# Output product by Strassen's seven quarter products in place of eight, on even and odd tokens, from column 512 on; x in a ring of block tiles

## The chip, the cores and the metric

One core of a Trainium2 chip. Its engines run side by side and meet through semaphores: TensorE (PE, with its weight loads PEld), VectorE (DVE), ScalarE (ACT), GpSimd (POOL) and SyncE (SP), which issues most transfers. The metric is the device time of one execution, in microseconds (us). Times given are medians of several runs.

## The reference

q, k and v are (8 batches, 8 heads, 576 positions, 64). A retention layer without a softmax gives x, 4608 tokens by 512, and a gated feed-forward layer gives the output, 4608 by 512 in float32:

```python
scores = scale * np.matmul(q, k.transpose(0, 1, 3, 2))
gamma = 1.0 - 2.0 ** (-5.0 - np.arange(H, dtype=np.float32))
Dmat = np.where(rel >= 0, gamma[:, None, None] ** rel[None, :, :], 0.0)   # rel = i - j
ret = scores * Dmat[None, :, :, :]
x = np.matmul(ret, v).transpose(0, 2, 1, 3).reshape(B * S, H * D)
gate = 1.0 / (1.0 + np.exp(-(x @ w_gate)))      # w_gate, w_val: 512 by 1536
val = x @ w_val
out = (gate * val) @ w_out                       # w_out: 1536 by 512
```

## The kernel before, in words

Matmuls take bf16 operands and add up in f32 in PSUM. x is held transposed, features on partitions and tokens along columns (`xT`). The kernel puts the tokens in an order of its own: a step of attention makes 128 columns of `xT`, and `rows` maps columns back to rows of the output.

The order of the work is written out by hand, and each engine's queue runs in that order. Columns 0 to 511 are made first, together with the loading and casting of the weights. From column 512 on a loop runs over `BLOCKS`: one of 256 columns, called block 512 after its first column, two of 384 (768 and 1152), and six of 512 (1536 to 4096). A block has two phases:

- *The hidden phase* (`h_units`). For each of 12 chunks of 128 hidden units, matmuls with `w_gate` and `w_val` (L734, four each) fill PSUM, ScalarE takes the sigmoid `g` (L748 in block 512, L758 after it), and VectorE multiplies to `gv` (L750, L762), which is bf16. The tiles come from `ffn_psum`, a ring of three banks: a chunk can start when the engine that reads the bank's old contents is done. In block 512 a chunk fills one bank, later it fills two.
- *The output phase* (`op_units`). For each 128 tokens, 12 matmuls of 512 columns with `wo_sb` (L801) add up in one bank; ScalarE copies it to `ob` (L777), and SP stores it later (L772). The last tile of the kernel is split in three parts (L791 to L796).

Between these units stands the attention of later columns. Up to block 1152 mostly single steps (`next_slot`) stand in the hidden phases; from there on double steps (`next_two`) stand in the output phases, at a fixed number of units from their start. A step has matmuls for its scores and state products (L519, L527) and for the values of an earlier step (L545, L561); VectorE masks the scores (L534), adds the states (L646, L642, L648) and, for single steps, adds one half of x (L633); ScalarE casts states (L495) and evacuates x (L603, L619). `glance` (L589) is a copy of one column, which makes TensorE's last value matmuls wait until VectorE has come to it. `pending` holds what is to follow a step, one entry per unit. In early block 512 a transpose on TensorE (L480) with copies on ScalarE and VectorE (L482) also stands; a copy of two small states (`sf`, L677) belongs to the fourth step.

q, k and v of later steps are loaded by SP in `ld_pool`, a ring of 18 buffers, and cast by GpSimd (L291, L296) at least three steps ahead of their use; most are then transposed by a transfer.

Of the kernel before, what the change touches and what calls it, by code (L numbers as in the profile page):

```python
# [9 lines left out]
FP32 = mybir.dt.float32  # L10
BF16 = mybir.dt.bfloat16
# [5 lines left out]
def kernel(  # L17
# [35 lines left out]
    att_pool = ctx.enter_context(tc.tile_pool(name="att", bufs=3))  # L53
    nat_pool = ctx.enter_context(tc.tile_pool(name="nat", bufs=5))
    consts = ctx.enter_context(tc.tile_pool(name="consts", bufs=1))

# [4 lines left out]
    st_psum = ctx.enter_context(tc.tile_pool(name="st_psum", bufs=1, space=PS))  # L61
    ffn_psum = ctx.enter_context(tc.tile_pool(name="ffn_psum", bufs=3, space=PS))

# [194 lines left out]

    xT = consts.tile([P, M, NT], BF16)


    natural = {}
# [171 lines left out]
    def third_out(apart):  # L434

        ps = pair_ps[5][0][0]
        share = nat_pool.tile([P, 2, P], FP32, tag="apart", name="apart", bufs=1)
        nc.vector.tensor_copy(out=share, in_=apart)
        nc.vector.tensor_tensor(out=xT[:, 0:2, 5 * P:6 * P], in0=ps[:, 0:2], in1=share, op=ALU.add)
        nc.scalar.copy(out=xT[:, 2:4, 5 * P:6 * P], in_=ps[:, 2:4])  # L440

# [23 lines left out]
    def pair_out(A, a, *engs):  # L465
        t0 = (2 * A + a) * P
        k = M // len(engs)
        for i, eng in enumerate(engs):
            ps, at_m, _ = pair_ps[2 * A + a][i * k]
            eng(out=xT[:, i * k:(i + 1) * k, t0:t0 + P], in_=ps[:, at_m:at_m + k])  # L470

# [127 lines left out]
    def after_two(vals, news, i):  # L599

        if i < NJ:
            for s in vals:
                nc.scalar.copy(out=xT[:, :, cols_of(s, i)], in_=val_ps[s][i])  # L603
        for n, s in enumerate(news):
            b, c = STEPS[s]
            if c == LAST:
                continue
            if i == n:
                add_state(s, 0)
                add_state(s, 1)  # L610
            if i == n + 1:
                for j in range(NJ):
                    if (s, j) in totals:
                        keep_state((b, c, j), totals.pop((s, j)), on_act)

    def leave_own(s, j):

        own = slice(2 * j, 2 * j + 2)
        nc.scalar.copy(out=xT[:, own, cols_of(s, j)], in_=val_ps[s][j][:, own])  # L619

# [6 lines left out]
    def leave_other(s, j):  # L627

        other = slice(2 - 2 * j, 4 - 2 * j)
        if before(s, j) is None:  # L630
            nc.vector.tensor_copy(out=xT[:, other, cols_of(s, j)], in_=val_ps[s][j][:, other])
        else:
            nc.vector.tensor_tensor(out=xT[:, other, cols_of(s, j)], in0=val_ps[s][j][:, other], in1=shares.pop((s, j)),  # L633
                                    op=ALU.add)

# [83 lines left out]
    def h_units(gvs, fcs, t0, a, e, banks=None):  # L719
# [6 lines left out]
        for i0 in range(0, len(fcs), k):  # L726
# [5 lines left out]
            def mm(out, w_sb, fc):  # L732
                for kc in range(NKC):
                    nc.tensor.matmul(out, lhsT=w_sb[:, kc, fc * P:(fc + 1) * P],  # L734
                                     rhs=xT[:, kc, t0 + a:t0 + e],
                                     start=(kc == 0), stop=(kc == NKC - 1))
# [32 lines left out]
    def leave():  # L769
        r, ob = stores.pop(0)  # L770
        for p0, r0, w in rows(r, P):
            nc.sync.dma_start(out[r0:r0 + w, :], ob[p0:p0 + w])  # L772

    def store(opp, r0, eng=None):

        ob = osb_pool.tile([P, DM], FP32, tag="osb", name=f"ob_{r0}")
        (eng or on_act)(out=ob, in_=opp)  # L777
        stores.append((r0, ob))
        if len(stores) > KEEP:
            leave()  # L780

    def op_units(gvs, t0, n):
        for nb in range(n // P):
            r0 = t0 + nb * P
            if r0 == NT - P:

                for i, (c0, w, queue, eng) in enumerate(((0, 256, nc.sync, on_act), (256, 128, nc.sync, on_dve),
                                                         (384, 128, nc.scalar, on_act))):
                    opp = ffn_psum.tile([P, w], FP32, tag="ffn", name=f"op_{t0}_{nb}_{i}")
                    for fc in range(NFC):  # L790
                        nc.tensor.matmul(opp, lhsT=gvs[fc][:, nb * P:(nb + 1) * P], rhs=wo_sb[:, fc, c0:c0 + w],  # L791
                                         start=(fc == 0), stop=(fc == NFC - 1))
                    ob = osb_pool.tile([P, w], FP32, tag="osb", name=f"ob_{r0}_{i}")
                    eng(out=ob, in_=opp)
                    for p0, at_row, n_row in rows(r0, P):
                        queue.dma_start(out[at_row:at_row + n_row, c0:c0 + w], ob[p0:p0 + n_row])  # L796
                    yield 12 * w
                return
            opp = ffn_psum.tile([P, 512], FP32, tag="ffn", name=f"op_{t0}_{nb}")
            for fc in range(NFC):  # L800
                nc.tensor.matmul(opp, lhsT=gvs[fc][:, nb * P:(nb + 1) * P], rhs=wo_sb[:, fc, :],  # L801
                                 start=(fc == 0), stop=(fc == NFC - 1))
                if fc % 4 == 3 and fc < NFC - 1:
                    yield 4 * 512
            store(opp, t0 + nb * P)
            yield 4 * 512

    def ffn_units(t0, n):
        gvs = {}
        yield from h_units(gvs, range(NFC), t0, 0, n)  # L810
        yield from op_units(gvs, t0, n)

# [17 lines left out]
    def h_both(fcs):  # L830

        gs = {}
        for what in ("g", "v"):
            for fc in fcs:
                pool, tag = (qk_psum, "qk") if what == "g" else (ffn_psum, "ffn")
                ps = pool.tile([P, 512], FP32, tag=tag, name=f"h{what}_0_{fc}")
                for kc in range(NKC):
                    nc.tensor.matmul(ps, lhsT=(wg_sb if what == "g" else wv_sb)[:, kc, fc * P:(fc + 1) * P],  # L838
                                     rhs=xT[:, kc, 0:4 * P], start=(kc == 0), stop=(kc == NKC - 1))
                if what == "g":  # L840
# [63 lines left out]
    def h_half(what, fc, x, ps):  # L904

        cols = slice(x * 256, x * 256 + 256)
        for kc in range(NKC):
            nc.tensor.matmul(ps, lhsT=(wg_sb if what == "g" else wv_sb)[:, kc, fc * P:(fc + 1) * P], rhs=xT[:, kc, cols],  # L908
                             start=(kc == 0), stop=(kc == NKC - 1))
# [120 lines left out]

    BLOCKS = [(512, 256), (768, 384), (1152, 384)] + [(t, 512) for t in range(1536, NT, 512)]
    SINGLE = [4, 3, 1]
# [3 lines left out]
    for w, (t0, n) in enumerate(BLOCKS):  # L1036
# [3 lines left out]
        begin = slots  # L1040
        total = 2 * NFC * 4 * n + 12 * 512 * (n // P)
        n_h = NFC if n <= 256 else 2 * NFC
# [9 lines left out]

        for i, cols in enumerate(ffn_units(t0, n)):
            gone += cols
            pieces += 1
# [6 lines left out]
            elif slots < end and gone * (end - begin) >= (slots - begin) * (total - 5 * 2048):  # L1062
                next_slot(slots)
                valued = slots - 1
                slots += 1
            elif twos and i - n_h >= (0 if len(twos) > 1 else 5 if n < 512 else 6):
                next_two(*twos[0])
                valued = twos[0][0][-1]
                slots = max([slots] + [s + 1 for s in twos.pop(0)[1]])
# [34 lines left out]
```

## Time and profile before

| | us |
|---|---|
| runs, median of 3 | 327.9 (327.29 to 328.12) |
| the profiled execution: span, the only time the page has of it | 325.9 |
| TensorE busy | 320.1 |
| VectorE busy | 148.9 |
| ScalarE busy | 140.6 |
| GpSimd busy | 103.8 |
| matmuls of the hidden phases (L734) | 2 x 100.7 |
| output matmuls from column 512 on (L801) | 84.0 |
| `gv` products (L762) | 62.8 |

The profile's rows read: line, engine, operation, output tile and input tiles, shapes, count, busy time and mean of one, then the engine's idle time before such instructions and who ended it. A row of a timeline starts with its start and its length; in square brackets is the idle time before it. The start is counted from the start of the span. A row of the chain has start and length, then engine and line. TensorE's matmuls are pipelined: its rows are longer than the step from one matmul to the next, so the price of a matmul is read from the start of one group to the start of the next.

### The profile page before, as it was taken

What the parts mean: (1) busy time and instruction counts of PE and PEld (TensorE: products, weight loads), DVE (VectorE), ACT (ScalarE), POOL (GpSimd) and SP (SyncE); (2) the same over time, 40 slices, a digit from 0 to 9 for tenths busy, and PEclk for the clock granted to TensorE, in tenths of its full rate; (3) what the DMA queues carried; (4) which work ended last, traced back from release to release, by engine and by line L of the source; (5) the groups of instructions that cost most, each with busy time, mean ns of one, the idle gap of its engine ahead of it and who ended that gap; (6) DMA issues with size and microseconds to landing.
All of it is one profiled execution on the core that took longest, in us unless ns stands there. A gap on an engine that the chain in (4) does not pass through costs nothing.

```text
span 325.9 us, 8785 instructions
## 1 busy us (share of the span) xinstructions
PE 320.1 (98%) x3630; PEld 170.0 (52%) x3630; DVE 148.9 (46%) x337; ACT 140.6 (43%) x316; POOL 103.8 (32%) x138
## 2 busy tenths in 40 slices
PE   8999999999999999999999999999999999999996
PEld 6664557856546554455445544454445544544444
DVE  6855466666606463355233534344344434404320
ACT  6755545555424353325432553335334533343322
POOL 5684536544465462028200830075003000000000
PEclk9999999999999999999999999999999999999999
DMA  7999999999999999509990899069804900010003
GB/s 224 331 365 389 383 243 211 196 170 171 222 212 205 242 247 204 142 2 227 201 219 0 177 231 241 2 141 203 210 0 120 345 25 0 34 67 33 3 32 97
DMA packets 145993, 55.14 MB, mean 169 GB/s; under 512 B 125216, under 2 KB 137888, under 8 KB 145952
## 3 DMA queue, kind: packets, MB, share of 16 engines
q1 hardware_dynamic: 145264, 54.25, 67.7%
q8 instruction: 28, 0.46, 0.5%
q10 hardware_dynamic: 688, 0.33, 0.3%
q14 instruction: 13, 0.11, 0.1%
HBM read 37.75 MB, written 9.44 MB: 145 GB/s over the span
## 4 chain that ended last, share of the span: by engine, by line
PE 94%; SPq 2%; DMA 2%; DVE 1%; issue 0%; ACT 0%; POOL 0%; ACTq 0%
PE h L734 51%; PE op L801 25%; PE op L983 3%; PE hg L838 3%; PE hv L838 3%; SPq L134 2%; PE val L545 2%; DMA v32p<-in_v_dram 2%; PE row L519 1%; PE row L527 1%; PE val L561 1%; PE op L791 1%; PE hv L908 1%; PE hg L908 1%; PE st L374 0%; PE turn L480 0%
## 5 line engine op out<-in xcount | busy, mean ns | idle before, releaser
L762 DVE TENSOR_TENSOR gv<-g,h 128x512 bf16<-128x512 bf16 (+1 forms) x96 | 62.8, 655 | 103.2 <-PE h L734 99.5
L734 PE MATMUL h<-xT,wv_sb 128*128 128x512 bf16 (+2 forms) x432 | 100.7, 356 | 0.0
L734 PE MATMUL h<-xT,wg_sb 128*128 128x512 bf16 (+2 forms) x432 | 100.7, 355 | 0.0
L758 ACT ACTIVATE g<-h 128x512 bf16<-128x512 f32 (+1 forms) x96 | 54.8, 570 | 94.3 <-PE h L734 90.1
L801 PE MATMUL op<-wo_sb,gv 128*128 128x512 bf16 x372 | 84.0, 379 | 0.0
L734 PEld LDWEIGHTS <-wg_sb 128*128 128x128 bf16 x432 | 41.9, 98 | 41.3 <-issue 0.2
L734 PEld LDWEIGHTS <-wv_sb 128*128 128x128 bf16 x432 | 41.9, 98 | 40.5
L801 PEld LDWEIGHTS <-gv 128*128 128x128 bf16 x372 | 35.3, 98 | 40.9
L296 POOL CAST v<-v 128x512 bf16<-128x512 f32 x29 | 17.9, 616 | 85.2 <-PE val L545 81.3
L291 POOL TENSOR_TENSOR qk<-k,ktab 128x512 bf16<-128x512 f32 x30 | 31.3, 1042 | 35.9 <-DMA k<-in_k_dram 32.4
L777 ACT COPY ob<-op 128x512 f32<-128x512 f32 x33 | 19.3, 585 | 35.5 <-PE op L801 34.5
L291 POOL TENSOR_TENSOR qk<-q,qtab 128x512 bf16<-128x512 f32 x28 | 29.2, 1042 | 4.3 <-DMA q<-in_q_dram 4.3
L534 DVE TENSOR_TENSOR pt<-row,tri 128x256 bf16<-128x256 f32 x60 | 21.6, 418 | 13.5 <-PE row L527 11.9
L603 ACT CAST xT<-val 128x256 bf16<-128x256 f32 x46 | 15.0, 380 | 22.7 <-PE val L561 19.6
L646 DVE TENSOR_TENSOR s<-s,row 128x256 f32<-128x256 f32 x39 | 16.3, 417 | 1.3
L495 ACT CAST sb<-s 128x256 bf16<-128x256 f32 x44 | 15.9, 420 | 0.7 <-DVE s L646 0.7
L589 DVE COPY glance<-val 128x1 f32<-128x1 f32 x24 | 2.7, 155 | 23.4 <-PE val L561 22.7
L983 PE MATMUL op<-wo_sb,gv 128*128 128x512 bf16 x48 | 11.7, 379 | 0.0
L545 PEld LDWEIGHTS <-v 64*64 64x64 bf16 x480 | 6.2, 108 | 7.5 <-issue 7.2
L561 PE MATMUL val<-T,sb 64*64 64x64 bf16 x368 | 9.8, 195 | 0.3 <-DVE glance L589 0.3
L519 PE MATMUL row<-T 64*64 64x64 bf16 x480 | 9.6, 196 | 0.0
L344 DVE TENSOR_TENSOR ptp<-qkp,trip 128x512 bf16<-128x512 f32 x12 | 7.6, 682 | 4.1 <-PE qkp L337 4.0
(107 smaller groups left out, 235.4 us busy)
## 6 DMA issues: line engine op xcount, KB each, us to landing
out_dram<-ob SPq DMA_DIRECT2D x31, 256.0 KB, 3.1
k<-in_k_dram SPq DMA_DIRECT2D x26, 256.0 KB, 3.9
q<-in_q_dram SPq DMA_DIRECT2D x26, 256.0 KB, 4.2
v<-in_v_dram SPq DMA_DIRECT2D x26, 256.0 KB, 4.4
wg<-in_moe_w_gate_dram SPq DMA_DIRECT2D x12, 256.0 KB, 5.2
wv<-in_moe_w_val_dram SPq DMA_DIRECT2D x12, 256.0 KB, 5.1
wo<-in_moe_w_out_dram SPq DMA_DIRECT2D x12, 256.0 KB, 5.5
v32p<-in_v_dram SPq DMA_DIRECT2D x6, 256.0 KB, 5.0
```

The source lines that it names most:

```text
L291: eng.tensor_tensor(out=natural_qk[s][:, i].rearrange("p m (y d) -> p y m d", y=2), in0=by_halves(loaded[s][1 - i]), in1=tab, op=ALU.mult)
L296: eng(out=natural["v", s], in_=loaded[s][2])
L495: eng(out=state[key], in_=src)
L534: nc.vector.tensor_tensor(out=probs[s][:, y], in0=row_ps[s][y][:, 0], in1=tri.unsqueeze(1).to_broadcast([P, M, 64]), op=ALU.mult)
L646: nc.vector.tensor_tensor(out=new, in0=running[b], in1=p, op=ALU.add)
L734: nc.tensor.matmul(out, lhsT=w_sb[:, kc, fc * P:(fc + 1) * P], rhs=xT[:, kc, t0 + a:t0 + e], start=(kc == 0), stop=(kc == NKC - 1))
L758: nc.scalar.activation(out=g[:, 0:n], in_=h1[:, 0:n], func=AF.Sigmoid)
L762: nc.vector.tensor_tensor(out=gvs[some[0]][:, a:e], in0=g[:, 0:n], in1=h2[:, 0:n], op=ALU.mult)
L777: (eng or on_act)(out=ob, in_=opp)
L801: nc.tensor.matmul(opp, lhsT=gvs[fc][:, nb * P:(nb + 1) * P], rhs=wo_sb[:, fc, :], start=(fc == 0), stop=(fc == NFC - 1))
L838: nc.tensor.matmul(ps, lhsT=(wg_sb if what == "g" else wv_sb)[:, kc, fc * P:(fc + 1) * P], rhs=xT[:, kc, 0:4 * P], start=(kc == 0), stop=( ...
L983: nc.tensor.matmul(opps[nb], lhsT=gvs[fc][:, nb * P:(nb + 1) * P], rhs=wo_sb[:, fc, :], start=(fc == 0), stop=(fc == NFC - 1))
```

## The change

For two tiles of 128 tokens the output is a product of `gv` (256 tokens by 1536) and `wo` (1536 by 512). The change halves all three dimensions: tokens into even and odd ones of a run of 256 or 512, hidden units into even and odd chunks, output columns into two halves of 256. Eight quarter products become seven, by Winograd's form of Strassen's scheme, with sums of quarters on both sides. Tiles that are left over (one in each block of 384) go through the old `op_units`.

- `wo_sums`: four sums of quarters of the weights, 1536 columns each, on VectorE, at units 0, 2, 4 and 6 of block 512.
- `gv_sums`: after each second chunk three dependent sums on VectorE and one on GpSimd, over 128 columns (256 in the blocks of 512), into a buffer from `ld_pool`.
- `quarters`: the products in the order 5, 1, 3, 6, 2, 7, 4, in two banks held for the whole time, `e` and `a`, each accumulated on in the bank or begun anew. ScalarE copies four partial sums out (`keep`), VectorE adds each bank to a copy and so writes `ob` (`add`).
- x is written with even tokens ahead of odd ones (`x_out`, `x_in`), and lives in a ring of four block tiles in place of one tile for all columns.
- stores write every second row, so one `ob` can take up to four transfers; the last product is split in two banks, stored from ScalarE's and SP's queues.
- double steps stand one unit later in the output phase.

The diff at its core:

```diff
+    wt_sb = consts.tile([P, 4, NFC // 2, DM // 2], BF16)
+    def wo_sums(i):
+        b11, b12, b21, b22 = (wo_sb[:, r::2, c:c + DM // 2] for r in range(2) for c in (0, DM // 2))
+        a, b = ((b12, b11), (b22, wt_sb[:, 0]), (b22, b12), (b21, wt_sb[:, 1]))[i]
+        nc.vector.tensor_tensor(out=wt_sb[:, i], in0=a, in1=b, op=ALU.subtract)
...
+    def x_out(rows_, cols):
+        if not dealt(cols):
+            return xT(rows_, cols)
+        t0, n = max(b for b in BLOCKS if b[0] <= cols.start)
+        at, w = (cols.start - t0) // 2, (cols.stop - cols.start) // 2
+        region = xT(rows_, slice(t0, t0 + n // 256 * 256)).rearrange("p m (r t) -> p m r t", r=2)
+        return region[:, :, :, at:at + w]
+
+    def x_in(x, cols):
+        return x.rearrange("p m (t r) -> p m r t", r=2) if dealt(cols) else x
...
-                nc.scalar.copy(out=xT[:, :, cols_of(s, i)], in_=val_ps[s][i])
+                nc.scalar.copy(out=x_out(ALL, cols_of(s, i)), in_=x_in(val_ps[s][i], cols_of(s, i)))
...
+    def gv_sums(gvs, fp, n):
+        t = ld_pool.tile([P, 4, 256], BF16, tag="ld", name="gsum")[:, :, 0:n]
+        a11, a21, a12, a22 = (gvs[2 * fp + o][:, h * n:(h + 1) * n] for o in range(2) for h in range(2))
+        nc.gpsimd.tensor_tensor(out=t[:, 2], in0=a11, in1=a21, op=ALU.subtract)
+        nc.vector.tensor_tensor(out=t[:, 0], in0=a21, in1=a22, op=ALU.add)
+        nc.vector.tensor_tensor(out=t[:, 1], in0=t[:, 0], in1=a11, op=ALU.subtract)
+        nc.vector.tensor_tensor(out=t[:, 3], in0=a12, in1=t[:, 1], op=ALU.subtract)
+        return t
...
+        def product(i, ps, first):
+            left, right = OF[i]
+            for fp in range(NFC // 2):
+                for b in range(k):
+                    nc.tensor.matmul(ps[:, b], lhsT=left(fp)[:, b * P:(b + 1) * P], rhs=right(fp),
+                                     start=(first and fp == 0 and b == 0), stop=(fp == NFC // 2 - 1 and b == k - 1),
+                                     skip_group_check=True)
+                if k > 1 and fp == NFC // 4 - 1:
+                    yield k * W * NFC // 4
...
+        def keep(name, ps):
+            kept[name] = sum_pool.tile([P, 2, W], FP32, tag="sum", name=f"s{name}_{t0}")[:, 0:k]
+            nc.scalar.copy(out=kept[name], in_=ps)
+
+        def add(b, c, ps, name):
+            ...
+            nc.vector.tensor_tensor(out=obs[b][:, c * W:(c + 1) * W], in0=ps, in1=kept[name][:, b % k], op=ALU.add)
...
+        e, a = held_bank("e"), held_bank("a")
+        yield from product(5, e, True)
+        keep("5", e)
+        yield tail
+        yield from product(1, a, True)
+        keep("1", a)
+        yield tail
+        yield from product(3, e, False)
+        keep("53", e)
+        yield tail
+        yield from product(6, a, False)
+        add_half(0, 1, a, "53")
+        yield tail
+        yield from product(2, e, True)
+        add_half(0, 0, e, "1")
+        ...
+        yield from product(7, a, False)
+        keep("7", a)
+        add_half(1, 1, a, "5")
+        if final:
+            for b in range(k, 2 * k):
+                send(b, 1, nc.sync)
+        ...
+        yield from product(4, e, True)
+        add_half(1, 0, e, "7")
...
+        for i, cols in enumerate(h_units(gvs, range(NFC), t0, 0, n)):
+            if i % 4 == 3 or n <= 256 and i % 2:
+                sums.append(gv_sums(gvs, len(sums), k * P))
+            yield cols
+        yield from quarters(gvs, sums, t0, k)
+        yield from op_units(gvs, t0, n, 2 * k)
...
+            if w == 0 and i in (0, 2, 4, 6):
+                wo_sums(i // 2)
...
-            elif twos and i - n_h >= (0 if len(twos) > 1 else 5 if n < 512 else 6):
+            elif twos and i - n_h >= (1 if len(twos) > 1 else 6 if n < 512 else 7):
```

Operands of the seven products (`raw` is a quarter of `gv`, `summed` a sum of such, `plain` and `mixed` the same for the weights):

```diff
+        OF = {1: (raw(0, 0), plain(0, 0)), 2: (raw(1, 0), plain(1, 0)), 3: (summed(3), plain(1, 1)),
+              4: (raw(1, 1), mixed(3)), 5: (summed(0), mixed(0)), 6: (summed(1), mixed(1)), 7: (summed(2), mixed(2))}
```

## The prediction

> **What bounds the kernel now.** I read the page's busy shares and its chain first, then TensorE's timeline for the price of a matmul by its width, then VectorE's timeline in block 512, where the change adds most to that queue, then the single groups for prices.
>
> ```profile
> span 325.9 us, 8785 instructions
> PE 320.1 (98%) x3630; PEld 170.0 (52%) x3630; DVE 148.9 (46%) x337; ACT 140.6 (43%) x316; POOL 103.8 (32%) x138
> PE 94%; SPq 2%; DMA 2%; DVE 1%; issue 0%; ACT 0%; POOL 0%; ACTq 0%
> ```
>
> TensorE is the bound: 94% of the chain. The sum is made against this execution's span, 325.9 us; the median of the runs, 327.9 us, is 2.0 above it, and the same difference is added at the end. The stretches of the chain, and the timeline, give the matmul's price and the last part:
>
> ```profile
> 55.91 1.75 PE h L734 x16
> 312.61 7.77 PE op L801 x36
> ...
> 320.22 2.81 PE L791 MATMUL op<-wo_sb,gv 128*128 128x256 bf16 x36
> 323.07 0.27 ACT L794 COPY ob<-op 128x128 f32<-128x128 f32 x1 [0.97 <-PE op L791]
> 323.36 0.37 ACTq L796 DMA_DIRECT2D out_dram<-ob  x1
> ```
>
> 16 matmuls of 256 columns in 1.75 us are 0.109 us each, 36 of 512 in 7.77 are 0.216. Two halves cost what one whole costs, each with its own weight load, so quarter products are not held up by width.
>
> VectorE's idle share, 54%, is an average. In block 512 it looks different (windows row, then its timeline):
>
> ```profile
> 48.00:70.00 22.00, 21.83 (x365) 15.60 (x363) 15.46 (x42) 11.84 (x36) 12.31 (x14) 1.00 1.07 196
> ...
> 52.88 0.42 DVE L750 TENSOR_TENSOR gv<-g,h 128x256 bf16<-128x256 bf16 x1 [1.46 <-ACT g L748]
> 53.22 0.75 DVE L534 TENSOR_TENSOR pt<-row,tri 128x256 bf16<-128x256 f32 x2
> 54.23 0.42 DVE L750 TENSOR_TENSOR gv<-g,h 128x256 bf16<-128x256 bf16 x1 [0.27 <-ACT g L748]
> 54.57 0.41 DVE L646 TENSOR_TENSOR s<-s,row 128x256 f32<-128x256 f32 x1
> ...
> 61.89 0.28 DVE L633 TENSOR_TENSOR xT<-val,share 128x128 bf16<-128x128 f32 x1
> 62.42 0.42 DVE L750 TENSOR_TENSOR gv<-g,h 128x256 bf16<-128x256 bf16 x1 [0.25 <-ACT g L748]
> ```
>
> The five numbers after the length are TensorE, weight loads, VectorE, ScalarE, GpSimd. VectorE is 70% busy there, GpSimd 56%, and between two `gv` products VectorE is idle some 0.3 to 0.5 us. TensorE waited 0.17 us for this very `xT` (L633) at 62.23. The queue is in order, and everything new stands in it.
>
> **The matmuls.** 15 pairs of 128-token tiles go from 24 matmuls of 512 columns to 42 of 256: 24 x 0.216 = 5.18 us against 42 x 0.109 = 4.59. Gain 0.59 us each, 8.9 us in all. All of it lies on the path. What follows is what TensorE newly waits for.
>
> **Block 512: the new VectorE work.** It gets 18 sums of 128 columns (three per pair of hidden chunks) and four sums of the output weights, 1536 columns each, all with both operands in bf16 in SBUF; the trace has no such instruction. Bounds for 128 columns: 0.155 us (L589, one column) and 0.284 (L633, f32, 128 columns). The bf16 copy L482 moves 512 columns in 0.42 us, what f32 needs for 256 (L646, 0.417), so I count half the columns: 0.22 us. For 1536: the f32 slope (0.688 - 0.284)/384 is 1.05 ns a column, 768 columns are 0.96 us; the ends are 0.42 (no shorter than 512 columns) and 1.77 (full rate).
>
> [...]
>
> An instruction of 0.42 us holds the queue 0.34 (52.88 to 53.22), one of 0.28 holds it 0.20; a dependent one starts some 0.06 after its predecessor's end. Up to the `xT` that TensorE's third attention slot waits for, the queue holds nine `gv`, four masks, four states and one copy (18 x 0.34), two `xT` (0.4): 6.5 us. New in front of it: four triples of dependent sums, 12 x 0.28 = 3.4 us, and four weight sums, 3.6 us. The first `gv` starts 1.55 us after the block's first matmul; 1.55 + 13.5 = 15.1 us against 10.8 before (62.17 - 51.33). The banks between allow three chunks of lead, which are used up: 4.3 us. Then the last `gv` and its sum hold the last matmul of the first product, 0.9 us, the next slot waits for two more `xT` behind sums, 0.4 us more than before, and a product of six matmuls (0.66 us) is too short for the copy or addition that frees its bank behind the state and `sf` copies: 1.2 us. Less the 0.6 gained: **+6.2 us**.
>
> GpSimd adds to it. L278 has two SBUF operands like the sums:
>
> ```profile
> 32.41 1.04 POOL L278 TENSOR_TENSOR kp<-k32p,ktab 128x512 bf16<-128x512 f32 x1 [0.85 <-DMA k32p<-in_k_dram]
> 33.10 0.90 DVE L278 TENSOR_TENSOR qp<-q32p,qtab 128x512 bf16<-128x512 f32 x1 [0.71 <-DMA q32p<-in_q_dram]
> ...
> 36.81 0.69 DVE L278 TENSOR_TENSOR qp<-q32p,qtab 128x512 bf16<-128x512 f32 x1
> ```
>
> Beside a GpSimd instruction with 0.35 us still to go it took 0.21 longer than alone. With GpSimd 56% busy in instructions of up to 1.04 us, 22 new ones lose at most 22 x 0.56 x (0.52 - 0.14) = 4.7 us, at least 0. I take 2.0, since sums in a row share a wait. **Block 512: +8.2.**
>
> **Blocks 768 and 1152** (one quartered pair and one plain tile each). The first product ends 6 x 0.109 = 0.66 us after the last hidden matmul, but `gv` (0.555), then its sum, are ready 0.6 us later than the last matmul wants them: that eats the 0.59. 768: 0.2 more for banks, **+0.2**. In 1152 two double attention steps are 5 products (3.3 us) apart where 20 matmuls (4.3 us) were; masks (4 x 0.34), states (4 x 0.45) and the additions are ahead of what frees the banks of products 7 and 4, 0.45 us each: **+1.0**.
>
> **Six blocks of 512.** Gain 1.18 each. The hidden phase hides its sums: a triple of 256 columns (0.28 to 0.42 each) fits in the 1.73 us between two `gv` of 0.69. Three waits remain. The first product reaches the last pair of chunks after 1.09 us, its sum is ready after about 0.3 + 0.69 + 0.3 + 0.1: 0.3 us. The glance (L589) of the second double step stands behind two additions, which wait for ScalarE's copy of the third product: 0.3. ScalarE's copy of product 7 stands behind four state casts (L495), which wait for VectorE's states, and holds the next block's first bank: 0.4. Net **-0.15** in the four full blocks (-0.6), **-0.5** in 3584, whose second step brings no new states, **-0.9** in 4096, which has none.
>
> **Reading with a stride.** Evacuations of `x` now take even and odd tokens apart. Between 0 and half of the 0.15 us by which `qT` (L328, 0.735, strided) exceeds `kT` (0.585); no gain, the elements are the same. I take 0; at the high end it moves the product 7 copy, 0.3 us in each of four blocks.
>
> **Stores and loads.** SP's queue gets 55 output transfers where 41 stood, 14 x 0.47 us (L772). Loads stand three steps ahead of use, which hides them; without that cover a late load would stop a slot, 0.6 us each. GpSimd's 54 new subtractions stand among the casts under the same cover. The ring of x tiles waits for readers three blocks back: 0.
>
> **The end.** The last copy was 128 columns on ScalarE (0.27), then one transfer, end 2.5 us after its issue. Now an addition of 256 columns (0.417), then three transfers in a row on SP (0.4 to 0.54 each), the third in place of the first, behind three of the tile's other half: **+1.3**.
>
> Sum: 8.2 + 0.2 + 1.0 - 0.6 - 0.5 - 0.9 + 1.3 = +8.7. Profiled 334.6, median **336.6 us**.
>
> **Rivals.**
> - *The gain comes through (faster).* If sums and weight sums fit into block 512's idle time, that is if the new 7.0 us up to the third slot cost under 2.7, only the end (1.3) and the waits in the first products (0.9 + 2 x 0.6 + 6 x 0.3 = 3.9) are left: -8.9 + 1.3 + 3.9 = -3.7, 324.2 us. For it: TensorE holds 94% of the chain. Against it: even at the lowest bounds (12 x 0.215 and 4 x 0.34) it is 3.9.
> - *Sums at full rate, or GpSimd in full.* Block 512 loses 10 to 13 us: 340 to 343 us. For it: L762's rate, L278's wait.
> - *Half of it.* Sums near 0.155, no wait for GpSimd, ScalarE's waits in the 512 blocks absent: block 512 +4.5, 512 blocks -5: about 329 to 332.
> - *The change does not do what it says.* Excluded: the changed program holds the 630 matmuls of 256 columns.
>
> **Chances.** Forecast (332 to 340) 0.58, full rate 0.18, half 0.14, faster 0.07, within 0.3% (1 us, which is what a measurement can tell here) 0.03. Slower 0.90. Leaving out the faster end and the top: 330.5 to 342.5; the likeliest alone 332 to 340.
>
> **What would show it.** TensorE idle in the first 12 hidden chunks of block 512, released by VectorE (`xT`, T or `gv`), 4 us or more; VectorE over 85% busy there; the weight sum at 0.96 us, the 128-column sum at 0.22; the period of a full 512 block, 33.9 us before, nearly unchanged; three transfers at the end. It would be wrong if the new sums were much cheaper than 0.155 + 0.06, or if the period of the 512 blocks fell by its full 1.2 us.

## The result, and the profile after

The changed kernel takes 353.1 us (median of 4, 352.6 to 354.4) against 327.9: 1.078 times the time before, 95% interval 1.076 to 1.081. Slower was forecast, at 332 to 340 us; the size, +25.3 us against +8.7, was not. The profiled execution after has a span of 352.7 us, so 26.8 us are to be explained.

The page's head and its chain, after:

```profile
span 352.7 us, 9627 instructions
PE 320.4 (91%) x3857; PEld 196.7 (56%) x3876; DVE 232.4 (66%) x562; ACT 141.8 (40%) x321; POOL 137.9 (39%) x192
PEclk9999999887999999999999999999999999999998
PE 53%; DVE 12%; issue 2%; ACT 2%; POOL 1%; DMA 1%; DVEq 0%; POOLq 0%; ACTq 0%
```

TensorE is busy as long as before, in spite of fewer columns, and its share of the chain fell from 94% to 53%; VectorE has 83.5 us more work, and its share of the chain rose from 1% to 12%. PEclk drops to 8, 8, 7 in slices 8 to 10 (62 to 88 us), most of which is block 512.

The length of a block is read from its first hidden matmul to that of the next block. In the last two columns stands what the prediction gave, and the same block when GpSimd's casts are replaced by zeros (experiment 1):

| us | before | after | more | predicted | with zeros |
|---|---|---|---|---|---|
| up to block 512 | 51.33 | 52.39 | +1.1 | 0 | +0.2 |
| 512 | 19.24 | 32.66 | +13.4 | +8.2 | +6.5 |
| 768 | 25.56 | 28.17 | +2.6 | +0.2 | +0.6 |
| 1152 | 26.55 | 27.59 | +1.0 | +1.0 | +1.0 |
| 1536 | 33.85 | 37.53 | +3.7 | -0.15 | +1.0 |
| 2048 | 33.94 | 34.47 | +0.5 | -0.15 | -0.1 |
| 2560 | 33.75 | 35.00 | +1.3 | -0.15 | +0.3 |
| 3072 | 33.91 | 35.42 | +1.5 | -0.15 | +1.0 |
| 3584 | 33.60 | 33.20 | -0.4 | -0.5 | -0.4 |
| 4096 and end | 34.17 | 36.27 | +2.1 | +0.4 | +2.1 |

The first row is no effect of the change: kernels here whose code is the same up to there start block 512 anywhere from 51.0 to 53.1 us.

Block 512 in the timeline, VectorE's sums (L846 to L848) beside GpSimd, and TensorE's wait for the `gv` behind them. The columns are start, length, engine, line:

```profile
56.65 1.04 POOL L343 TENSOR_TENSOR qk<-k,ktab 128x512 bf16<-128x512 f32 x1
56.80 0.97 DVE L847 TENSOR_TENSOR gsum<-gsum,gv 128x128 bf16<-128x128 bf16 x1
57.65 1.04 POOL L343 TENSOR_TENSOR qk<-q,qtab 128x512 bf16<-128x512 f32 x1
57.81 0.97 DVE L848 TENSOR_TENSOR gsum<-gv,gsum 128x128 bf16<-128x128 bf16 x1
...
59.03 0.41 DVE L806 TENSOR_TENSOR gv<-g,h 128x256 bf16<-128x256 bf16 x1
...
59.49 0.60 PE L790 MATMUL h<-xT,wg_sb 128*128 128x256 bf16 x4 [1.64 <-DVE gv L806]
...
61.28 0.22 DVE L846 TENSOR_TENSOR gsum<-gv,gv 128x128 bf16<-128x128 bf16 x1
61.54 0.23 DVE L847 TENSOR_TENSOR gsum<-gsum,gv 128x128 bf16<-128x128 bf16 x1
```

With no cast beside it a sum takes 0.22 to 0.23 us, as predicted. (GpSimd's casts of q and k, L343, multiply by a table and so read two tiles; the cast of v, L348, reads one.) Beside a cast of 1.04 us it takes 0.97 here, and each sum of a dependent row ends just after the cast that ran beside it (57.77 after 57.69, 58.78 after 58.69). The casts stand back to back, so when the next sum starts (57.81) the next cast is already under way (57.65): one cast per sum, not one per row. Grouped over block 512 the eighteen sums take 11.1 us of VectorE's queue instead of 4.1. The groups' last columns are busy time, and mean ns of one:

```profile
L847 DVE TENSOR_TENSOR gsum<-gsum,gv 128x128 bf16<-128x128 bf16 x6 | 4.3, 720 | 0.2
L846 DVE TENSOR_TENSOR gsum<-gv,gv 128x128 bf16<-128x128 bf16 x6 | 3.8, 640 | 0.4
L848 DVE TENSOR_TENSOR gsum<-gv,gsum 128x128 bf16<-128x128 bf16 x6 | 3.0, 496 | 0.2
```

TensorE's own rows show a second loss in the same block:

```profile
62.41 0.32 PE L599 MATMUL val<-pt,v 64*64 64x64 bf16 x14 [1.75 <-DVE T L536]
...
63.31 1.04 PE L790 MATMUL h<-xT,wg_sb 128*128 128x256 bf16 x4
64.13 1.06 PE L790 MATMUL h<-xT,wv_sb 128*128 128x256 bf16 x4
64.99 1.06 PE L790 MATMUL h<-xT,wg_sb 128*128 128x256 bf16 x4
...
76.55 0.40 PE L884 MATMUL qe<-wt_sb,gsum 128*128 128x256 bf16 x1 [2.56 <-DVE gsum L846]
76.73 1.49 PE L884 MATMUL qa<-wo_sb,gv 128*128 128x256 bf16 x6
...
79.71 1.46 PE L884 MATMUL qe<-wo_sb,gsum 128*128 128x256 bf16 x6
80.97 1.49 PE L884 MATMUL qa<-wt_sb,gsum 128*128 128x256 bf16 x6
```

From 63.31 to 64.99 eight matmuls step at 0.21 us, where the price is 0.109, and again from 76.7 to about 83. Each time TensorE had been idle shortly before: 1.64 and 1.75 us, then 2.56. In the same trace the granted clock is 0.50 from 62.6 to 66.0 us and from 76.3 to 83.1, and 1.00 in between. Over the whole block it is 0.84 (windows row; TensorE, weight loads, VectorE, ScalarE and GpSimd follow the length, the clock is third from the end):

```profile
52.39:85.05 32.66, 23.86 (x364) 18.43 (x363) 28.77 (x64) 11.50 (x36) 21.18 (x25) 0.84 0.98 195
```

The excess over 0.109 in these matmuls adds up to about 3.5 us. VectorE is 88% busy.

In a block of 512 the cast meets the one sum that TensorE needs:

```profile
232.92 0.67 POOL L845 TENSOR_TENSOR gsum<-gv 128x256 bf16<-128x256 bf16 x1 [2.79 <-DVE gv L818]
233.54 1.04 POOL L343 TENSOR_TENSOR qk<-k,ktab 128x512 bf16<-128x512 f32 x1
...
234.59 1.14 DVE L846 TENSOR_TENSOR gsum<-gv,gv 128x256 bf16<-128x256 bf16 x1
...
235.79 0.39 PE L884 MATMUL qe<-wt_sb,gsum 128*128 128x256 bf16 x2 [0.99 <-DVE gsum L846]
```

GpSimd's own subtraction of the last pair waits for the eleventh `gv`; the casts stand behind it in GpSimd's queue, start when it is done, and run just when the last sum is wanted.

At the end, from just before the end of the last matmul (346.74), seven transfers leave on one queue, one after another, until 350.15:

```profile
346.55 3.60 SPq L913 DMA_DIRECT2D out_dram<-ob  x7
```

### The profile page after: what moved, and what is told of

It is laid out like the page before. It is cut to its first block, busy times and chain, and to the rows that moved or that the text cites. A ratio compares the mean times of both kernels' runs of the same rounds, so it can differ in the third digit from the quotient of the medians.

```text
span 352.7 us, 9627 instructions
## 1 busy us (share of the span) xinstructions
PE 320.4 (91%) x3857; PEld 196.7 (56%) x3876; DVE 232.4 (66%) x562; ACT 141.8 (40%) x321; POOL 137.9 (39%) x192
## 4 chain that ended last, share of the span: by engine, by line
PE 53%; DVE 12%; issue 2%; ACT 2%; POOL 1%; DMA 1%; DVEq 0%; POOLq 0%; ACTq 0%
PE h L790 38%; PE qa L884 6%; PE qe L884 5%; DVE ob L901 3%; DVE gv L818 3%; DVE gsum L846 2%; PE op L964 1%; DVE s L702 1%; DVE gsum L847 1%; DVE pt L588 1%; PE val L599 1%; ACT s L896 1%; DMA out_dram<-ob 1%; PE val L615 1%; POOL qk L343 1%
## 5 line engine op out<-in xcount | busy, mean ns | idle before, releaser
L818 DVE TENSOR_TENSOR gv<-g,h 128x512 bf16<-128x512 bf16 (+1 forms) x96 | 62.6, 653 | 51.1 <-PE h L790 49.3
L845 POOL TENSOR_TENSOR gsum<-gv 128x256 bf16<-128x256 bf16 (+1 forms) x54 | 33.7, 626 | 158.7 <-DVE gv L818 152.6
L884 PEld LDWEIGHTS <-gsum 128*128 128x128 bf16 x360 | 35.0, 99 | 16.2 <-DVE gsum L846 9.5
L343 POOL TENSOR_TENSOR qk<-k,ktab 128x512 bf16<-128x512 f32 x30 | 31.4, 1047 | 11.5 <-DMA k<-in_k_dram 11.3
L343 POOL TENSOR_TENSOR qk<-q,qtab 128x512 bf16<-128x512 f32 x28 | 29.9, 1067 | 0.7 <-DMA q<-in_q_dram 0.5
L884 PEld LDWEIGHTS <-gv 128*128 128x128 bf16 x258 | 25.0, 100 | 5.8 <-issue 2.2
L901 DVE TENSOR_TENSOR ob<-qa,s 128x256 f32<-128x256 f32 x30 | 11.6, 420 | 22.7 <-PE qa L884 8.6
L846 DVE TENSOR_TENSOR gsum<-gv,gv 128x256 bf16<-128x256 bf16 (+1 forms) x54 | 21.1, 390 | 4.3 <-DVE gv L818 0.5
L884 PE MATMUL qa<-wt_sb,gsum 128*128 128x256 bf16 x180 | 23.3, 277 | 0.2 <-DVE ob L901 0.2
L847 DVE TENSOR_TENSOR gsum<-gsum,gv 128x256 bf16<-128x256 bf16 (+1 forms) x54 | 21.9, 406 | 1.8
L348 POOL CAST v<-v 128x512 bf16<-128x512 f32 x29 | 18.2, 628 | 9.2 <-PE val L599 4.9
L848 DVE TENSOR_TENSOR gsum<-gv,gsum 128x256 bf16<-128x256 bf16 (+1 forms) x54 | 18.4, 341 | 1.8
L884 PE MATMUL qe<-wt_sb,gsum 128*128 128x256 bf16 x90 | 13.0, 275 | 7.0 <-DVE gsum L846 6.8
L896 ACT COPY s<-qe 128x512 f32<-128x512 f32 (+1 forms) x18 | 9.4, 521 | 22.6 <-PE qe L884 22.6
```

The source lines that it names most:

```text
L343: eng.tensor_tensor(out=natural_qk[s][:, i].rearrange("p m (y d) -> p y m d", y=2), in0=by_halves(loaded[s][1 - i]), in1=tab, op=ALU.mult)
L348: eng(out=natural["v", s], in_=loaded[s][2])
L818: nc.vector.tensor_tensor(out=gvs[some[0]][:, a:e], in0=g[:, 0:n], in1=h2[:, 0:n], op=ALU.mult)
L845: nc.gpsimd.tensor_tensor(out=t[:, 2], in0=a11, in1=a21, op=ALU.subtract)
L846: nc.vector.tensor_tensor(out=t[:, 0], in0=a21, in1=a22, op=ALU.add)
L847: nc.vector.tensor_tensor(out=t[:, 1], in0=t[:, 0], in1=a11, op=ALU.subtract)
```

## The experiments

Theory A: VectorE's sums and GpSimd's casts hold each other up, and this, with what follows from it, is the excess over the prediction. Theory B: VectorE's queue is too long by itself. Theory C: the matmuls at half rate are a large part of block 512.

### 1. GpSimd writes zeros in place of its casts

The casts of the steps are left out, and with them what GpSimd reads for them; its subtractions stay.

```diff
+        if eng is nc.gpsimd:
+            nc.gpsimd.memset(natural_qk[s][:, i], 0.0)
+            return
...
+        if eng == on_pool:
+            nc.gpsimd.memset(natural["v", s], 0.0)
+            return
```

> The changed kernel, in which GpSimd fills the natural q, k and v tiles of the steps with zeros where it cast them before: the casts are left out, the transfers and everything else stay, and x of those steps is zero. GpSimd then writes these tiles and reads nothing. Theory A (VectorE's sums and GpSimd's casts hold each other up: in the changed kernel 128-column sums beside a 1.04 us cast take 0.97 to 1.03 us, alone 0.23): the excess over the prediction goes, with what follows from it. Block 512 falls from 32.7 us to 25 to 27 (19.24 before, +6.2 of VectorE's queue alone), the last sum of the 512 blocks from 1.02 to 1.15 us to about 0.29, and the whole from 353.1 to 334 to 340 us. Theory B (VectorE's queue is too long by itself, GpSimd or not): the sums stay above 0.5 us, block 512 stays above 31 us, the whole above 349 us.

> The kernel before with the same zeros in place of GpSimd's casts, as control: the casts are left out. Both theories: no VectorE work of the old kernel stands long beside the casts on TensorE's path (TensorE idles 0.17 us there), so 327 to 328.5 us, block 512 at 19.0 to 19.3 us. If this kernel falls by as much as the changed one, the zeros' shorter time itself, not the sums, is what a_writes shows.

Measured: 340.1 us for the changed kernel (1.037, interval 1.034 to 1.040), 328.0 for the kernel before (1.000, 0.999 to 1.001). The 340.1 is at the upper edge of theory A's range. Block 512 is 25.70 us, the others stand in the table above. So the casts cost the changed kernel 13 us and the old one nothing; of the span's 14.6 us, 7.0 are in block 512, 2.0 in 768, 2.7, 0.6, 1.0 and 0.5 in the four full blocks, and the rest is the start. This is theory A, for about half of the loss: without the casts the changed kernel is still 12 us slower than the kernel before, and 6.5 of these stand in block 512.

One doubt is left: a memset of 0.5 us is half as long as a cast. So each q and k tile was then filled twice:

```diff
+            for _ in range(2):
+                nc.gpsimd.memset(natural_qk[s][:, i], 0.0)
```

> The changed kernel with zeros in place of GpSimd's casts, as in a_writes (the casts are left out), but each q and k tile is filled twice, 2 x 0.5 us where its cast took 1.04, so that GpSimd is as busy as with the casts and still reads nothing. Theory A (what holds the sums up is GpSimd's reading of SBUF beside sums that read two operands there): block 512 stays at 25.7 us, the 128-column sums at 0.23 us, the whole at 339.5 to 341 us. Rival (it is GpSimd's busy time: the casts in a_writes were simply twice as short, GpSimd 10.7 us busy in block 512 against 21.2, and its own subtractions came sooner): block 512 goes back to 29 to 32 us, the whole to 346 us or more.

Measured: 340.8 us (1.039, 1.030 to 1.048), block 512 at 25.85. GpSimd is busy 14.3 us of it, 55%, against 65% with the casts. So it is not quite as busy, but the rows stand side by side:

```profile
60.22 2.15 POOL L344 MEMSET qk<- 128x512 bf16 x4
60.35 0.22 DVE L853 TENSOR_TENSOR gsum<-gv,gv 128x128 bf16<-128x128 bf16 x1
...
60.61 0.23 DVE L854 TENSOR_TENSOR gsum<-gsum,gv 128x128 bf16<-128x128 bf16 x1
...
60.87 0.23 DVE L855 TENSOR_TENSOR gsum<-gv,gsum 128x128 bf16<-128x128 bf16 x1
```

Three dependent sums run beside 2.15 us of writing at the price they have alone. It is the reading that collides here, not GpSimd's being busy: in block 512 a sum takes 0.90 to 1.03 us beside casts of 1.04, which read, and 0.22 to 0.23 beside memsets, which only write.

### 2. Without the sums of the output weights

```diff
         def mixed(i):
-            return lambda fp: wt_sb[:, i, fp]
+            return lambda fp: wo_sb[:, 2 * fp, (i % 2) * W:(i % 2 + 1) * W]
...
-            if w == 0 and i in (0, 2, 4, 6):
-                wo_sums(i // 2)
```

> The changed kernel without the four sums of the output weights: the products take plain quarters in their place, so this part of the computation is left out. Only block 512 changes. By the prediction's term (3.6 us of VectorE's queue up to the third slot's xT) block 512 falls by 3.6 us, from 32.7 to 29.1. Theory A: the narrow dependent sums, not these, meet the casts, so block 512 falls by 3 to 4.5 us and stays above 28 us. Theory C (idle TensorE loses its clock, 0.213 us per 256-column matmul at 63.3 to 66.3 and 76.7 to 83.3 us, some 4 us in all, and the weight sums are what makes it idle): it falls by 6 to 8 us and those matmuls step at 0.109.

> The changed kernel with zeros in place of GpSimd's casts and without the weights' sums, both at once; the casts are left out and the products take plain quarters in place of the sums. Block 512 is 32.7 us in the changed kernel, 25.7 with the zeros, 30.0 without the weights' sums. By the prediction's terms, which had the two as separate sums, 25.7 less 3.6: 22.1 us. Theory A with the clock: the matmuls at 0.205 to 0.215 us, which a_writes still has at 66.9 to 70.2 us, are gone as well, 20.5 to 22 us. If the weights' sums were hidden beside other waits, it stays above 24 us.

Measured: alone 350.0 us (1.067, 1.064 to 1.071), block 512 from 32.66 to 30.04; with the zeros as well 335.6 us (1.024, 1.021 to 1.026), block 512 from 25.70 to 21.63. With the casts in place removing them gives 2.6 us, less than the prediction's 3.6, a little less than the 3 to 4.5 of theory A, and far less than theory C's 6 to 8: TensorE still waits for `gv`, T and sums, and still has 12 matmuls at 0.21 from 60.4 us and 30 from 75.0. With the casts gone it gives 4.1 us, and the clock with it:

```profile
51.39:73.02 21.63, 19.52 (x363) 16.08 (x362) 17.20 (x60) 11.35 (x36) 8.14 (x18) 1.00 1.09 197
```

In a_writes itself 0.93 was granted, and some 1.5 us went on matmuls at half rate after waits of 1.77 and 0.35 us; an earlier wait of 1.46 us, by itself, had left the matmuls at 0.109. In a_writes_no_w, with no wait above 0.7 us in the block, no matmul runs at half rate. So here the half rate follows the waits: it makes them dearer, and it is not what starts them.

### 3. Another order of the products

The order 1, 2, 6, 5, 7, 3, 4 needs no sum of `gv` in its first two products.

```diff
-        e, a = held_bank("e"), held_bank("a")
-        yield from product(5, e, True)
-        keep("5", e)
-        yield tail
+        a, e = held_bank("a"), held_bank("e")
         yield from product(1, a, True)
         keep("1", a)
...
+        yield from product(2, e, True)
+        add_half(0, 0, e, "1")
...
         yield from product(6, a, False)
+        keep("16", a)
```

> The changed kernel with its products in the order 1, 2, 6, 5, 7, 3, 4 and the banks to match, so that no sum of gv is needed in the first two products, and with the last tile's stores ordered so that the very last is one transfer on ScalarE's queue. Same casts, same sums. Theory A: what the casts make of the sums is hidden where two products (2.6 us in a 512 block, 1.3 in block 512) lie in front of it. The wait in the first product goes (0.4 to 1.0 us in each of the four full 512 blocks), block 512 loses the 2.56 us wait at 76.55 and the half-rate matmuls behind it (about 3 us), its hidden phase (20.9 us against 13.2 before) stays; the end loses 1.5 us of its 5.96: 353.1 falls to 343 to 346 us. Theory B: the same sum is only late at another place, the wait moves to product 6 or 5, and the whole stays above 349 us.

Measured: 349.8 us (1.067, 1.062 to 1.073). That is the figure of this run's theory B, by which the same sum is only late at another place. Block 1536 gained 2.6 us, but block 512 only 1.5 where about 3 was expected. In the full blocks the wait in the first product went, and another stood in its place:

```profile
228.65 1.05 POOL L343 TENSOR_TENSOR qk<-k,ktab 128x512 bf16<-128x512 f32 x1
...
229.65 1.05 POOL L343 TENSOR_TENSOR qk<-q,qtab 128x512 bf16<-128x512 f32 x1
229.69 1.15 DVE L846 TENSOR_TENSOR gsum<-gv,gv 128x256 bf16<-128x256 bf16 x1
...
230.87 0.58 DVE L847 TENSOR_TENSOR gsum<-gsum,gv 128x256 bf16<-128x256 bf16 x1
...
231.49 1.01 DVE L848 TENSOR_TENSOR gsum<-gv,gsum 128x256 bf16<-128x256 bf16 x1
...
232.43 0.21 DVE L643 COPY glance<-val 128x1 f32<-128x1 f32 x2
...
232.69 0.32 PE L615 MATMUL val<-T,sb 64*64 64x64 bf16 x16 [1.53 <-DVE glance L643]
```

The three sums take 2.74 us beside the casts where they take 0.29 each alone, and the glance of the next attention step stands behind them in VectorE's queue. The end did not improve either: 6.3 us from the last matmul, since the rows of the other half tiles were left for SP's queue after the last ones.

### 4. Quarters from column 1536 on, and the casts moved

```diff
+    def pairs_of(t0, n):
+        return n // 256 if t0 >= 1536 else 0
```

(used wherever the kernel had `n // 256`; the weights' sums then stand in block 1152). It was run first by itself, then with the new order, then also with the fourth subtraction on VectorE:

```diff
-        nc.gpsimd.tensor_tensor(out=t[:, 2], in0=a11, in1=a21, op=ALU.subtract)
         nc.vector.tensor_tensor(out=t[:, 0], in0=a21, in1=a22, op=ALU.add)
+        nc.vector.tensor_tensor(out=t[:, 2], in0=a11, in1=a21, op=ALU.subtract)
```

> The changed kernel with quarter products from column 1536 on only; blocks 512, 768 and 1152 are plain as before, and the weights' sums stand in block 1152. Theory A and the periods read in the changed kernel: the blocks of 512 cost what they cost there (37.5, 34.5, 35.0, 35.4, 33.2 and 36.3 us against 33.9, 33.9, 33.8, 33.9, 33.6 and 34.2 before, +8.6 in all; the first less, some 2, if part of its +3.7 was left over from block 1152), and the early blocks are back at 19.2, 25.6 and 26.6: 335 to 337 us. Rival (the slow early blocks push the loads and casts of the later ones into their way): the later blocks recover too, 329 to 332 us.

> The same with the products in the order 1, 2, 6, 5, 7, 3, 4. Where the sums stood in front of the first product they now stand in front of the glance of the first double step (1.4 to 1.5 us in each 512 block of the kernel with the new order alone): blocks of 512 at 34.2 to 34.9 us, the end as there, 332 to 335 us by theory A. Theory B (VectorE's queue by itself): the same.

> The same, and GpSimd's own subtraction of each pair of chunks goes to VectorE, at 0.3 us each. GpSimd's casts of the next steps then no longer stand behind a subtraction that waits for the tenth gv, and start when their loads land, in the hidden phase. Theory A (the 1.5 us wait is there because the casts start at the very moment of the last sums): the glance waits 0.3 us or less, the blocks fall to 33.0 to 33.6 us, 326 to 329 us in all. Theory B: one more sum per pair makes VectorE's queue longer, the glance waits 1.5 us or more, 333 to 336 us.

Measured: 335.4 us (1.023, 1.019 to 1.026), 333.7 (1.018, 1.015 to 1.021) and 328.0 (1.000, 0.999 to 1.001). The first shows that the later blocks lose by themselves: they stay at 34.9 to 35.4 us with the early ones back at their old length. Block 1536, at 34.75 in place of 37.53, had most of its +3.7 us from the blocks before it. The second was expected at 332 to 335 by both theories. The third separates A from B: one more sum for VectorE makes the kernel 5.7 us faster, block 2560 goes from 34.83 to 33.13, and the wait of 1.5 us for the glance is gone. GpSimd and VectorE at that place:

```profile
213.76 0.29 DVE L848 TENSOR_TENSOR gsum<-gv,gv 128x256 bf16<-128x256 bf16 x1
213.97 0.28 DVE L849 TENSOR_TENSOR gsum<-gv 128x256 bf16<-128x256 bf16 x1
...
214.18 0.28 DVE L850 TENSOR_TENSOR gsum<-gsum,gv 128x256 bf16<-128x256 bf16 x1
...
214.50 0.29 DVE L851 TENSOR_TENSOR gsum<-gv,gsum 128x256 bf16<-128x256 bf16 x1
214.53 0.73 POOL L351 CAST v<-v 128x512 bf16<-128x512 f32 x1 [19.59 <-PE val L602]
```

The time came as theory A had it, but the way there was not the one it named. Only two casts moved up into the hidden phase (at 192.9); the third waited 19.6 us for value matmuls of TensorE (by the profile), held the rest back, and all of these started once the last sum had begun, instead of running through beside the sums of the hidden phase. So the gain shows the same cause, casts and sums apart in time, but it hangs on where that one cast stands.

### 5. The end, and what is left

s1536_all sends each half tile of the last block as soon as it is written, on two queues. s1536_all2 also puts ScalarE's copy of product 7 ahead of VectorE's additions, cuts the weights' sums into halves, and sends whole rows of the last but one tile:

```diff
-        def send(b, c, queue):
-            for at, to in places(b):
-                queue.dma_start(out[to, c * W:(c + 1) * W], obs[b][at, c * W:(c + 1) * W])
+        def send(b, c, *queues):
+            for i, (at, to) in enumerate(places(b)):
+                queues[i % len(queues)].dma_start(out[to, c * W:(c + 1) * W], obs[b][at, c * W:(c + 1) * W])
...
-        add_half(1, 1, a, "5")
-        keep("7", a)
+            keep("7", a)
+            add_half(1, 1, a, "5")
```

> The same, and in the last block the stores of each half tile are issued as soon as it is written and dealt out on ScalarE's and SP's queues, where twelve stood on SP's queue behind each other. From the last matmul to the end 3 us or less in place of 6 (2.87 before): 2.5 to 3.5 us less than the run without it, 323 to 326 us. If the landing of many small transfers rather than their issue on one queue is what takes the time, the tail stays above 5 us.

> s1536_all with ScalarE's copy of product 7 ahead of VectorE's additions (TensorE waits 0.4 us for it in each of five blocks), the weights' sums in eight halves in place of four (block 1152 is 27.06 us with four, 26.55 before), and fewer transfers on SP's queue at the end (4.4 us from the last matmul to the end, 2.87 before). Each as read: 1.8, 0.4 and 0.9 us less, 325.9 to about 322.8 us. If the waits only change their place, 325 to 326.5 us.

Measured: 325.9 us (0.994, 0.992 to 0.996) and 324.8 us (0.990, 0.988 to 0.993). The last is 0.9% faster than the kernel before; about 322.8 had been expected of it. From the last matmul to the end it is 7.2 us without these changes and 4.4 with either, where 3 and then 3.5 were expected. In the last kernel four transfers follow each other on ScalarE's queue up to 1.6 us after the last matmul, and the end comes 2.8 us after that. The halves gave their 0.4 us (block 1152 at 26.66). The copy gave 0.1 to 0.2 us in three of the four full blocks instead of 0.4; the fourth, block 2048, is 0.4 us longer than in s1536_all, of which 0.3 is a wait for nothing that the profile shows (0.55 in place of 0.27). At the last product TensorE no longer waits for the copy, but up to 0.2 us for ScalarE's state casts.

The same changes, but with quarter products from column 512 on:

> The changed kernel from column 512 on, with the order 1, 2, 6, 5, 7, 3, 4, all four subtractions of a pair on VectorE, ScalarE's copy of product 7 ahead of VectorE's additions, and the stores of the last block dealt out on two queues. Theory A: from 1536 on every full block of 512 takes 33.0 to 33.3 us, as in s1536_all; blocks 512, 768 and 1152 still have the casts beside their sums, 28 to 31, 26 to 28.5 and 27 to 28 us: 335 to 341 us, so the loss that is left lies in the small blocks. Rival (once the casts are no longer behind GpSimd's subtractions, they run ahead in the small blocks too): block 512 at 25 us, 330 to 332 us.

Measured: 340.7 us (1.039, 1.034 to 1.045). From 1536 on the full blocks take 33.1 to 33.8 us; blocks 512, 768 and 1152 take 30.4, 29.5 and 28.7. So the rival fell: in the small blocks casts run beside sums in this order too. Blocks 768 and 1152 lie above the range of theory A (up to 28.5 and 28), and above the 28.2 and 27.6 of the changed kernel: the edits that win in the full blocks lose about 1 us in each of these two. Why was not tried apart.

## Why the prediction was wrong

What held:

- *The matmuls.* 24 x 0.216 against 42 x 0.109: from the first hidden matmul of block 4096 to its last matmul it takes 30.31 us in place of 31.30, -1.0 (predicted -0.9). Block 3584 comes to -0.4 (-0.5). These are the two blocks in which GpSimd casts nothing.
- *The sums' own prices.* 0.22 us predicted and 0.225 measured for 128 columns, 0.29 for 256 (0.28 to 0.42), 0.95 for a weight sum (0.96). Half the columns is what these rows show too: a bf16 sum of 256 columns takes 0.29 us, where one of 128 columns with f32 operands took 0.284 (L633 of the kernel before).
- *VectorE's queue in block 512, +6.2.* Without the casts it is +6.5, and without the weight sums too +2.4, so the term of 3.6 for them measures 4.1. That the totals agree so well is in part luck, since the inside was different: 4.3 us of waits (1.8, 1.5, 0.7 and 0.3) and 1.5 us of matmuls at half rate, for which the sum had no term. The 4.1 has these 1.5 in it.
- *Block 1152*, +1.0, with casts and without.

What failed:

- *"GpSimd adds to it ... I take 2.0, since sums in a row share a wait", with 4.7 as the upper bound.* This is the step that sank the forecast. They do not share it: when the next dependent sum starts, GpSimd's next cast is already under way, and each sum waits until its cast is done. It measures 7.0 us in block 512 (about 2 of them matmuls at half rate behind the longer waits), above even the bound. And it was counted there alone, while 768 (2.0) and the full blocks (2.7, 0.6, 1.0, 0.5) pay it too: 13.8 us in place of 2.0. The bound took a share of busy time and an average rest of a cast, as if the two queues met by chance. But the casts stand back to back, and behind a sum that one cast held up the next cast is there at once.
- *"The hidden phase hides its sums" and 0.3 us for the first product's last sum in the blocks of 512.* This wait is 1.0 us in three of the four full blocks and 0.3 in 2048, because GpSimd's new subtraction holds the casts back until that moment. "GpSimd's 54 new subtractions stand among the casts under the same cover" looked at whether casts are late for the steps, and not at what they are beside.
- *ScalarE's copy of product 7, 0.4 us at the next block's first bank.* The wait there is 0.3 to 1.0 us, and it is VectorE's additions behind that copy that end the wait. Even without the casts the four full blocks lose 2.2 us where -0.6 was predicted.
- *No term for the clock.* Matmuls at half rate are about 3.5 us of block 512's 13.4; they follow the waits, so without the casts 1.5 are left.
- *The end, +1.3.* It measures +3.1 (5.97 us from the last matmul to the end in place of 2.87). Seven transfers of 0.51 us go down one queue in a row. The prediction named six of them, three of the last half tile behind three of the other; its 1.3 is about what the longer addition (0.15) and two transfers more come to, and leaves next to nothing for those ahead of them. With the matmuls' -1.0 this is the last row's +2.1.

Of the rivals, the one with "GpSimd in full" was of the right kind, and its 343 us still too low. (By the prediction's own sum, a loss of 10 to 13 us in block 512 gives 338.4 to 341.4, not 340 to 343.)

Open is one wait of block 1536: TensorE stands 1.5 us in product 1 for nothing that the profile shows. It was not tried apart. With the zeros 0.8 us of it is left, and in s1536, where the block comes after plain ones, it is not there. Just before it, from 165.96 to 167.34, a packet of the trace's instruction queue is under way, and the wait begins at 167.34; whether the two belong together is not shown.

## What to carry to other kernels

Before a VectorE instruction with two operands in SBUF is added, look in the timeline at what GpSimd reads at that moment: here each 128-column sum of a dependent row took up to 1.03 us beside casts of 1.04, and 0.22 to 0.23 alone, while `gv`, with one operand in PSUM, kept its 0.41 beside a cast (at 55.82 in the changed kernel). It helped to move the two apart in time (5.7 us from s1536_order to s1536_order_t2) or to let GpSimd only write (13 us in a_writes). A new instruction in an engine's queue also decides when the work behind it starts, so follow that work to what it will run beside. Where TensorE will idle, look at its granted clock behind the wait: in the changed kernel it was 0.50 for 3.4 us behind waits of 1.64 and 1.75 us, which doubled the price of a matmul to 0.21, and 1.00 behind 1.78 and 0.34.

## What was not expected of the hardware

- The hold-up works both ways. GpSimd's 128-column subtraction takes 0.43 us alone and 1.08 beside a weight sum of 0.95, and a cast that takes 1.04 alone took 1.61 (both in the changed kernel):

```profile
54.28 0.95 DVE L282 TENSOR_TENSOR wt_sb<-wo_sb 128x1536 bf16<-128x1536 bf16 x1
54.52 1.61 POOL L343 TENSOR_TENSOR qk<-q,qtab 128x512 bf16<-128x512 f32 x1 [0.53 <-DMA q<-in_q_dram]
...
62.60 0.95 DVE L282 TENSOR_TENSOR wt_sb<-wo_sb 128x1536 bf16<-128x1536 bf16 x1
62.77 1.08 POOL L845 TENSOR_TENSOR gsum<-gv 128x128 bf16<-128x128 bf16 x1 [1.51 <-DVE gv L806]
```

- Matmuls fell to half rate (0.21 us in place of 0.109) behind short waits: in a_no_w behind 0.92 and 0.80 us within 2.9 us, but not behind 1.46 us by itself in a_writes:

```profile
57.53 0.60 PE L782 MATMUL h<-xT,wg_sb 128*128 128x256 bf16 x4 [0.92 <-DVE gv L798]
...
59.51 0.34 PE L591 MATMUL val<-pt,v 64*64 64x64 bf16 x14 [0.80 <-DVE T L528]
...
60.41 1.04 PE L782 MATMUL h<-xT,wg_sb 128*128 128x256 bf16 x4
```

The slow stretches measured 3.4 us or twice that (62.6 to 66.0 and 76.3 to 83.1 in the changed kernel by its clock, 66.6 to 70.0 in a_writes by its matmuls). The length of the waits alone did not decide: behind 1.77 and 0.35 us close together matmuls ran at half rate in a_writes, while 1.78 and 0.34 us (at 70.33 and 70.89 in the changed kernel) left the clock at 1.00. The longest single wait of TensorE in block 512 is 2.56 us. What sets the clock is not shown.

- Writing with GpSimd cost VectorE's sums nothing: 0.22 to 0.23 us each, as alone, beside four memsets that last 2.15 us together (a_writes_twice).
